# GateLoop attention and a maxout feed-forward block on one core: a shorter conversion of the weights, joined sums, constant biases, and new order lists

## The chip, the cores and the metric

The kernel runs on one core of a Trainium2 chip. The metric is the device time of one execution in microseconds. All arithmetic is in 32-bit floating point. A core has a matrix engine (TensorE, PE in the profile), three elementwise engines (VectorE or DVE, ScalarE or ACT, GpSimd or POOL) and SyncE (SP), which here only issues transfers. Transfers run on 16 DMA engines; they are issued from SP's queue and, where the transfer adds to its destination, from POOL's.

## The reference

Two blocks follow each other. The first is a gated linear recurrence over 768 steps for 4 batches and 8 heads of width 48, with complex gates:

```
mag = sqrt(a_re*a_re + a_im*a_im)
scale = minimum(mag, 0.999) / (mag + 1e-06)
a_re_n, a_im_n = a_re*scale, a_im*scale
for t in range(S):
    S_re, S_im = ar*S_re - ai*S_im + k_t (x) v_t, ar*S_im + ai*S_re
    y[:, :, t] = q_t . S_re
```

The second takes y as 3072 rows of 384 features:

```
h = maximum(maximum(x @ w1, x @ w2), x @ w3)      # 384 -> 768
out = h @ w_out                                    # 768 -> 384
```

The four weight matrices arrive as 64-bit floating point numbers.

## The kernel before, in words

The work is cut into 12 groups of 128 time steps, each for two batches (`g` 0 to 11; `x` and `y` at the end of a word name the two batches). Per group the kernel goes through these stages.

- Gates (`gates`, line 503): from the loaded `a_re` and `a_im` (words `Lr`, `Li`) the logarithm of the clamped size (`Ln`) and the angle (`w`) are made by a chain of ScalarE and VectorE words: `sqr sqi add lnL expw expe lne relu Lnop abs addw lnw expL mulai mulw stt xor half atan turn`. For group 0 they run in two halves (`sqr0`, `sqr1` and so on). `Lnop` and `addw` add one tile to another.
- Angles (`angles`, 586): `cs` is a prefix sum over time by TensorE, `t`, `nf`, `af` reduce it to one turn, `sa` and `sb` are the sines, `Cd` carries the last row into the next group by a transfer that adds.
- Turns and factors (`turns`, 622; `factors`, 687): sums of `Ln` (`sums`), their exponentials (`Ek`, `Eq`, `En`), the turned keys and queries (`uk`, `uq`), their transposes on TensorE (`tpk`, `tpq`) and copies out (`Kc`, `Qc`), per-block decay factors (`F`, `f0` to `f3`, `Q1`, `Q2`, `KB`, `QB`, `QG`, `kEn`).
- Scores, state and output of the recurrence (`scores`, 718; `state`, 770; `outputs`, 805): `A`, `B` and the picks `g0` to `g3`, `b0`, `b1`; `dk` and the state updates `h0` to `h3`; `y` and its copy `x` (`xx`, `xy`).
- Feed-forward: for groups 1 to 11 `U01 U11 U02 U12` are four stages of matrix products and `u..` the maxima (`up`, 862), and the second product is done with seven half-size products (`seven`, 897): sums `S1` to `S4` of blocks of h, products `P1` to `P7`, `Px`, `Py`, and the sums `r1 r6 r5 r7 r57 ox oy` into the output tile `ot`. Group 0 does both plainly in smaller pieces (`U01x`, `O`, `o`).

Ahead of the first feed-forward stage the weights are converted from 64 to 32 bits in 12 blocks of 384 KB (`weight_step`, 431). Block `i` is loaded raw (`WLi`), each number as two 32-bit words, and goes through the steps a (ScalarE: size of the high word, scaled), b (VectorE: an upper limit), c (VectorE: shift left by 3, in blocks 0, 3 and 6 with an or besides), e (VectorE: the upper bits of the low word or'ed in) and f (VectorE: the sign from the high word). `Wg` (blocks 1, 2, 4, 5, 7, 8) subtracts block w1 from w2 and w3 by an addition. `T`, `t`, `M`, `m` form a product of two weights; `J1` to `J4` prepare the seven products.

The order of all work is written out by hand in three lists. `SCHEDULE` (line 21) is one list of words `name:group`; each engine gets its instructions in the order of that list, and a class `Bound` (201) ties every instruction to the one in front of it on its engine. Because every instruction passes through `Bound`, the profile gives line L210 for nearly all of them, so groups are told apart by tile names. `SLOTS` (127) gives for each PSUM tile one of four double banks, in order (`banks`, 220). `OTHER` (134) names the words that are done on the second of two possible engines: a copy or size or relu or maximum on VectorE in place of ScalarE (`copy` 241, `magnitude` 248, `larger` 854), and an addition (`increase`, 255: `Lnop`, `addw`, `Wg`) on VectorE in place of an adding transfer from POOL's queue. `activation` (229) loads another table set on ScalarE whenever a word needs the set that isn't loaded: one set has the exponential and the logarithm, the other sine and arctangent. All tiles that live in turns come from tile pools with two buffers (`ldx`, `nat2`, `un2`, `fp2`, lines 189 to 194). Biases of activations stand in a tile `biases`.

Of the kernel before, what the change touches and what calls it, by code (L numbers as in the profile page):

```python
# [26 lines left out]
turn1:0 Lry:1 sqr:1 t1:0 WL11:0 Lkx:0 tx:0 nfx:0 Wa11:0 Wb10:0 csy:0 afx:0 sax:0 mkx:0 Wb11:0 Wc10:0 Lix:1 sbx:0
uqx:0 sqi:1 Lix:2 Wc11:0 Lky:0 tpqx:0 ty:0 add:1 f3x:0 f2x:0 ukx:0 Fy:0 Qcx:0 We10:0 Wf10:0 nfy:0 tpkx:0 We11:0
lnL:1 WL2:0 Q2x:0 kEnx:0 Eqy:0 expe:1 Eky:0 relu:1 xor:1 expw:1 QBx:0 Kcx:0 abs:1 T2:0 T0:0 t0:0 CL:0 KBx:0 WL1:0
Wa1:0 pw:1 Q1x:0 mky:0 Wb1:0 f0y:0 f1y:0 Wc1:0 t2:0 f2y:0 Wf11:0 lne:1 Lnop:1 Ax:0 g0x:0 Lry:2 g1x:0 We1:0 g2x:0  # L30
half:1 Lqy:0 Cdx:0 f3y:0 Liy:2 Lvx:0 mqy:0 Wa2:0 Wb2:0 lnw:1 expL:1 M0:0 mulw:1 Wc2:0 M1:0 mulai:1 dkx:0 Wf1:0
# [5 lines left out]
Wb7:0 Wg4:0 U11x:0 xor:2 By:0 dky:0 U02x:0 Lvx:1 b1y:0 h1y:0 b0y:0 QGy:0 yy:0 addw:2 lnw:2 expL:2 xy:0 U11y:0 Wg5:0
u02x:0 U02y:0 afx:1 half:2 u11x:0 Wc7:0 lne:2 We7:0 mulw:2 mulai:2 sbx:1 h2y:0 Z4:0 sax:1 h3y:0 stt:2 atan:2 Wf7:0
U12x:0 u12x:0 say:1 sby:1 Cdy:1 WL8:0 Cdx:1 turn:2 ukx:1 uqx:1 U01y:0 u01y:0 u11y:0 Wa8:0 U12y:0 csy:2 ty:2 u12y:0
csx:2 tpqx:1 tx:2 u02y:0 Qcx:1 nfy:2 Lnop:2 nfx:2 tpkx:1 Fy:1 kEnx:1 Wb8:0 Wc8:0 We8:0 Kcx:1 Wg7:0 Wf8:0 U21y:0  # L40
Wg8:0 KBx:1 f0y:1 u21y:0 Lky:1 Lqy:1 mky:1 afy:2 sumsx:2 dkx:1 Q1x:1 f1y:1 f2y:1 f3y:1 Enx:2 U21x:0 u21x:0 afx:2
# [10 lines left out]
xx:2 By:2 u02:1 Ay:2 S1:1 nfy:3 relu:4 tx:3 expe:4 S2:1 expw:4 P5:1 P6:1 g0y:2 afy:3 say:3 sby:3 nfx:3 sbx:3 g1y:2
afx:3 sax:3 abs:4 dky:2 P1:1 Lqy:3 g2y:2 g3y:2 b1y:2 J4:0 QGy:2 P7:1 Px:1 P2:1 b0y:2 h0y:2 h1y:2 ukx:3 tpkx:3 lne:4
Lnop:4 r1:1 Liy:5 mky:3 h2y:2 h3y:2 S4:1 Kcx:3 uqx:3 yy:2 Lqx:4 kEnx:3 mqy:3 tpqx:3 Qcx:3 P3:1 r6:1 xy:2 Py:1 r5:1
r7:1 P4:1 Fy:3 uky:3 r57:1 f0y:3 f1y:3 xor:4 half:4 oy:1 ox:1 Q1x:3 addw:4 dkx:3 h1x:3 Lvy:3 f2y:3 f3y:3 h0y:3
h2x:3 sumsx:4 Ekx:4 h3x:3 lnw:4 QGx:3 expL:4 Eqx:4 Fx:4 KBx:3 U11:2 Dx:1 QBx:3 mulai:4 Q2x:3 f2x:4 Enx:4 u11:2
# [88 lines left out]
def kernel(  # L145
# [15 lines left out]
    P = 128  # L161
# [881 lines left out]
```

## Time and profile before

| what | value |
|---|---|
| time, median of 3 runs | 561.11 us (557.43 to 561.78) |
| span of the profiled execution | 556.9 us |
| TensorE busy | 524.6 us |
| VectorE busy | 490.4 us in 770 instructions |
| ScalarE busy | 370.0 us |
| GpSimd busy | 74.4 us |

The span is counted from the first to the last instruction of one profiled execution; the three runs were timed apart from it and lie 0.5 to 4.9 us above it. In the lines that follow a group reads: line, engine, operation, destination tile <- source tiles, shape, count, then busy time in us and the mean of one in ns, then the idle time of the engine just before them and what ended it. In the table of stretches each engine has its busy time and its number of instructions; then come TensorE's granted clock, the mean busy share of the DMA engines and GB/s.

### The profile page before, as it was taken

To read this page: it belongs to the slowest core of one execution; us is meant where nothing else is said; L and a number is where in the kernel's file an instruction comes from. 1 tells how busy PE (TensorE), PEld (TensorE's weight loads), DVE (VectorE), ACT (ScalarE), POOL (GpSimd) and SP (SyncE) were. 2 spreads that over 40 slices of the span, in tenths; PEclk is the share of its full clock that TensorE was granted. 3 is DMA by queue.
4 is the path that set the end of the run, shared out by engine and by line. 5 is a ranking of instruction groups with operands and counts; after the bars stand their busy time and mean duration, and the time that the engine had idled before them with its cause. 6 is when DMAs were issued, how large, how long until landed. Compare 5 with 4: busy or idle time off the path is not lost.

```text
span 556.9 us, 22739 instructions
## 1 busy us (share of the span) xinstructions
PE 524.6 (94%) x10086; PEld 449.0 (81%) x10086; DVE 490.4 (88%) x770; ACT 370.0 (66%) x652; POOL 74.4 (13%) x117
## 2 busy tenths in 40 slices
PE   1669799989999999999999999999999999999997
PEld 0356588778888898888988888988888888998986
DVE  5999999989998899999988897999999999886524
ACT  5999989867965867787766858777646855530100
POOL 8105250002030001000120200120010020000000
PEclk9869999999999999999999999999999999999999
DMA  8977976456055164235364136542361144000000
GB/s 218 287 191 156 206 154 102 78 105 123 18 108 109 21 123 77 48 63 92 68 115 82 33 61 121 110 88 50 58 126 31 32 88 82 10 31 2 7 25 29
DMA packets 142530, 49.09 MB, mean 88 GB/s; under 512 B 130528, under 2 KB 135648, under 8 KB 142432
## 3 DMA queue, kind: packets, MB, share of 16 engines
q1 hardware_dynamic: 136272, 37.77, 31.9%
q0 software_dynamic: 6160, 9.87, 10.4%
q8 instruction: 79, 1.29, 1.0%
q14 instruction: 19, 0.16, 0.1%
HBM read 33.03 MB, written 4.72 MB: 68 GB/s over the span
## 4 chain that ended last, share of the span: by engine, by line
PE 84%; DVE 6%; DMA 4%; SPq 2%; issue 1%; ACT 1%; POOL 0%; DVEq 0%
PE up L210 34%; PE op L210 24%; PE y L210 7%; PE A L210 5%; PE tp L210 4%; PE dk L210 4%; PE sums L210 3%; PE cs L210 2%; SPq L210 2%; DMA xhx<-in_moe_w_out_dram 2%; PE F L210 2%; DVE xhx L210 1%; PE B L210 1%; DMA k<-in_k_dram 1%; DMA ar<-nf 1%
## 5 line engine op out<-in xcount | busy, mean ns | idle before, releaser
L210 PE MATMUL up<-xhx,w 128*128 128x256 f32 x792 | 177.4, 382 | 0.1
L210 PEld LDWEIGHTS up<-xhx,w 128*128 128x128 f32 x792 | 148.6, 190 | 21.5 <-PE B L210 0.3
L210 ACT ACT_TABLE_LOAD x45 | 57.7, 1283 | 1.5 <-PEq L1027 0.8
L210 ACT COPY atm<-B 32x128 f32<-32x128 f32 x96 | 24.5, 255 | 36.9 <-DVE atm L210 22.9
L210 PE MATMUL op<-wo,xhx 128*128 128x192 f32 (+1 forms) x220 | 48.5, 364 | 0.0
L210 DVE TENSOR_TENSOR Q<-Q,f 112x1024 f32<-112x1024 f32 (+1 forms) x48 | 45.4, 950 | 0.8 <-ACT Q L210 0.6
L210 ACT ACTIVATE f<-F 48x232 f32<-48x232 f32 x96 | 34.4, 359 | 13.2 <-PE F L210 5.4
L210 POOL DMA_DIRECT2D ar<-nf x40 | 34.2, 1280 | 65.3 <-DVE ar L210 54.7
L210 PE MATMUL y<-atm,vb 128*32 128x64 f32 x1152 | 39.4, 221 | 1.4 <-issue 1.1
L210 PEld LDWEIGHTS op<-wo,xhx 128*128 128x128 f32 x220 | 36.5, 190 | 4.3 <-DVE q L210 0.3
L210 POOL DMA_DIRECT2D Ln<-e x11 | 11.1, 1005 | 214.6 <-ACT e L210 53.9
L210 PE MATMUL y<-QG,g 112*32 112x64 f32 x1408 | 38.4, 219 | 0.9 <-issue 0.8
L210 PEld LDWEIGHTS y<-atm,vb 128*32 128x32 f32 x1152 | 32.5, 109 | 6.4 <-issue 3.6
L210 PEld LDWEIGHTS y<-QG,g 112*32 112x32 f32 x1408 | 34.8, 109 | 1.3 <-issue 1.0
L210 DVE TENSOR_TENSOR ot<-ot,op 128x192 f32<-128x192 f32 (+1 forms) x67 | 27.1, 413 | 9.0 <-PE op L210 4.3
L210 PE MATMUL op<-wo,strassen 128*128 128x192 f32 x176 | 33.0, 331 | 0.0
L210 PE MATMUL A<-Q,K 112*32 112x80 f32 x1536 | 31.6, 234 | 1.3 <-DVE Q L210 1.3
L210 DVE COPY_PREDICATED atm<-masko,A 128x256 f32<-128x256 uint8 x72 | 31.2, 435 | 1.6
L210 PE MATMUL op<-w,strassen 128*128 128x192 f32 x176 | 32.5, 329 | 0.0
L210 PEld LDWEIGHTS A<-Q,K 112*32 112x32 f32 x1536 | 27.2, 110 | 5.0 <-issue 1.9
L210 ACT COPY Q<-tp 112x1024 f32<-112x1024 f32 x23 | 23.3, 1013 | 10.3 <-PE tp L210 10.0
L210 ACT COPY ot<-op 128x192 f32<-128x192 f32 (+1 forms) x13 | 4.5, 342 | 38.2 <-PE op L210 38.2
(151 smaller groups left out, 1120.8 us busy)
## 6 DMA issues: line engine op xcount, KB each, us to landing
ar<-in_a_re_dram SPq DMA_DIRECT2D x24, 192.0 KB, 3.7
ai<-in_a_im_dram SPq DMA_DIRECT2D x24, 192.0 KB, 3.8
q<-in_q_dram SPq DMA_DIRECT2D x96, 48.0 KB, 2.6
k<-in_k_dram SPq DMA_DIRECT2D x96, 48.0 KB, 2.9
vb<-in_v_dram SPq DMA_DIRECT2D x96, 48.0 KB, 3.1
out_dram<-ot SPq DMA_DIRECT2D x23, 192.0 KB, 2.8
Ln<-e POOLq DMA_DIRECT2D x11, 384.0 KB, 4.7
w<-L POOLq DMA_DIRECT2D x9, 384.0 KB, 4.7
```

Source lines behind the costliest of these rows:

```text
L210: ins = f(*a, **kw)
```

## The change

Five things change at once.

1. The conversion of a weight block has four steps in place of five. Step b comes first and limits the high word from both sides on VectorE, reading it from the raw block; step a is then a Prelu on ScalarE that scales positive and negative numbers by different powers of two, so that the sign ends in the top bit after the shift; c is the plain shift; e writes the destination; f is gone.
2. The sums `r5` and `r7` become one instruction `r75` over both halves.
3. The biases of sine, relu and logarithm are given as constants; the tile `biases` keeps one column.
4. The tiles of the pools `ldx`, `nat2`, `un2` and `fp2` become fixed pairs, chosen by the batch. `Ek` and `Eq`, which shared one pair, get a pair each.
5. `SCHEDULE`, `SLOTS` and `OTHER` are new from the first word to the last. The new list has 1880 words (1903 before). It begins with the second half of group 0, and the constants `CL` stand first. In `OTHER`, `Lnop` of the groups 1, 3, 6, 8 and 11 and `Wg4` are new, so these additions move from POOL's transfers to VectorE; `relu:1`, `abs:1`, `afx:0`, `xx:0`, `u21x:0`, `relu:3` move from ScalarE to VectorE, and further on some copies `Kc` and `Qc`, while others go the other way.

The lists cut to the stretch that the prediction speaks of, and the code:

```diff
 SCHEDULE = """
-Lrx:0 Lix:0 sqi0:0 WL0:0 sqr0:0 xor0:0 add0:0 Wa0:0 Wb0:0 Wc0:0 We0:0 Liy:0 Wf0:0 lnL0:0 expw0:0 expe0:0 relu0:0
...
-Bx:1 KBy:1 kEny:1 lne:3 Ox:0 Eky:2 b1x:1 Eny:2 QBy:1 b0x:1 h0y:1 ukx:2 By:1 Eqy:2 yx:1 g3y:1 xx:1 b1y:1 Lqy:2 mqy:2
-Lvx:2 ox:0 Lky:2 mky:2 b0y:1 tpkx:2 expw:3 Kcx:2 uqx:2 Lnop:3 uqy:2 tpqx:2 Qcx:2 QGy:1 dky:1 h1y:1 kEnx:2 sumsx:3
-uky:2 Ekx:3 h2y:1 Eqx:3 Enx:3 yy:1 xy:1 Fy:2 f3y:2 h3y:1 dkx:2 f2y:2 abs:3 KBx:2 h0x:2 h1x:2 Q1x:2 f0y:2 f1y:2
-U11:1 u11:1 tpky:2 Kcy:2 Lky:3 QBx:2 QGx:2 addw:3 Lqx:3 h2x:2 mqx:3 h3x:2 xor:3 half:3 Cdx:2 tpqy:2 Qcy:2 Q2x:2
...
+CL:0 Zf:0 Liy:0 sqi1:0 Lry:0 sqr1:0 add1:0 lnL1:0 expe1:0 expw1:0 relu1:0 lne1:0 Lnop1:0 WL0:0 Lrx:0 Wb0:0 Lix:0 WL6:0
...
+sqr:3 tpqx:2 Qcx:2 f0x:2 U22x:0 Ay:1 By:1 dky:1 add:3 g0y:1 u22x:0 Ox:0 lnL:3 expw:3 expe:3 mky:2 g1y:1 g2y:1 relu:3
+h1y:1 uky:2 h2y:1 g3y:1 b1y:1 abs:3 lne:3 ukx:2 J1:0 QBx:2 Lnop:3 h3y:1 b0y:1 ox:0 Lry:4 Dy:0 Lvx:3 Lrx:4 Lky:3 Lqy:3
+Lvx:2 tpkx:2 tpky:2 tpqy:2 yy:1 Qcy:2 Kcy:2 xor:3 Kcx:2 Q2x:2 addw:3 h0x:2 kEny:2 Q1x:2 half:3 sumsy:3 Fy:2 xy:1 f3y:2
+Eky:3 f2y:2 lnw:3 Eqy:3 expL:3 f0y:2 mulai:3 mulw:3 sqi:4 QGx:2 stt:3 sqr:4 Eny:3 atan:3 Cdx:2 Cdy:2 kEnx:2 U11:1 u11:1
...
+P3:11 r75:11 ox:11 P4:11 r57:11 oy:11 Dx:11 Dy:11
...
-        if step == "a":
-            activation(out=ex.bitcast(FP), in_=high.bitcast(FP), func=AF.Abs, scale=2.0 ** -112)
-        elif step == "b":
-            dve.tensor_single_scalar(out=ex.bitcast(FP), in_=ex.bitcast(FP), scalar=LAST, op=OP.min)
+        if step == "b":
+            dve.tensor_scalar(out=ex.bitcast(FP), in0=high.bitcast(FP), scalar1=LAST, scalar2=-LAST, op0=OP.min,
+                              op1=OP.max)
+        elif step == "a":
+            activation(out=ex.bitcast(FP), in_=ex.bitcast(FP), func=AF.Prelu, alpha=-2.0 ** 32,
+                       scale=-2.0 ** -112 if i in (0, 3, 6) else 2.0 ** -112)
         elif step == "c":
-            if i in (0, 3, 6):
-                dve.tensor_scalar(out=ex, in0=ex, scalar1=3, scalar2=-0x80000000, op0=OP.logical_shift_left,
-                                  op1=OP.bitwise_or)
-            else:
-                dve.tensor_single_scalar(out=ex, in_=ex, scalar=3, op=OP.logical_shift_left)
+            dve.tensor_single_scalar(out=ex, in_=ex, scalar=3, op=OP.logical_shift_left)
         elif step == "e":
-            dve.scalar_tensor_tensor(out=ex, in0=low, scalar=29, in1=ex, op0=OP.logical_shift_right, op1=OP.bitwise_or)
-        elif step == "f":
-            dve.scalar_tensor_tensor(out=dst.bitcast(I32), in0=high, scalar=-0x80000000, in1=ex,
-                                     op0=OP.bitwise_and, op1=OP.bitwise_xor)
+            dve.scalar_tensor_tensor(out=dst.bitcast(I32), in0=low, scalar=29, in1=ex, op0=OP.logical_shift_right,
+                                     op1=OP.bitwise_or)
...
-                activation(out=e, in_=e, func=AF.Ln, scale=1e-6 * math.exp(-LNMAX), bias=least)
+                activation(out=e, in_=e, func=AF.Ln, scale=1e-6 * math.exp(-LNMAX), bias=math.exp(-LNMAX))
...
-            E = T[name, x] = nat2.tile([P, DM], FP, tag=name[:1 + (n == 1)], name=name[:1 + (n == 1)])
+            E = T[name, x] = es[name][c]
...
+                if name == "r75":
+                    two_ = ot.rearrange("p c n -> p (c n)")[:, NH:3 * NH].rearrange("p (u n) -> p u n", u=2)
+                    again = yl.rearrange("p (u n) -> p u n", u=1).to_broadcast([P, 2, NH])
+                    dve.tensor_tensor(out=two_, in0=again, in1=ps[:, 1, 0:DM].rearrange("p (u n) -> p u n", u=2), op=OP.add)
+                    return
```

More of the change, by code (lines that the diff above doesn't have):

```diff
@@ L27 @@
[L27 to L31, printed above, removed]
@@ L37 @@
[L37 to L41, printed above, removed]
@@ L52 @@
[L52 to L56, printed above, removed]
@@ L107 @@
-afy:10 Eqy:10 Lqy:10 dky:9 P5:8 tx:10 lne:11 P6:8 P7:8 Ay:9 h0y:9 nfx:10 h1y:9 By:9 QGy:9 h2y:9 h3y:9 g0y:9 sbx:10
-g1y:9 g2y:9 relu:11 afx:10 sax:10 ukx:10 g3y:9 P1:8 S4:8 r1:8 say:10 sby:10 mqy:10 r6:8 r5:8 r7:8 b0y:9 b1y:9
-expw:11 Py:8 P4:8 r57:8 Px:8 uqx:10 yy:9 xy:9 Fy:10 abs:11 f2y:10 Lky:10 oy:8 tpkx:10 kEnx:10 tpqx:10 f0y:10 f1y:10
-f3y:10 uqy:10 Qcx:10 Lnop:11 P2:8 Dy:8 mky:10 Kcx:10 Q1x:10 addw:11 QGx:10 Lvx:10 P3:8 ox:8 U11:9 QBx:10 u11:9
-sumsx:11 Enx:11 sumsy:11 half:11 uky:10 tpqy:10 Ekx:11 Q2x:10 Eqx:11 Lkx:11 tpky:10 Qcy:10 Kcy:10 Q2y:10 mkx:11
@@ new lines @@
+h2y:9 r6:8 r75:8 S4:8 r57:8 h3y:9 QGy:9 oy:8 sumsy:10 Fy:10 Fx:10 P2:8 P3:8 addw:11 Eqy:10 Eky:10 uqx:10 xor:11 ukx:10
+mky:10 f2x:10 f1x:10 Eny:10 mqy:10 uqy:10 ox:8 f3x:10 f3y:10 lnw:11 f0x:10 yy:9 xy:9 expL:11 f0y:10 f1y:10 tpkx:10
+tpqx:10 Qcx:10 Lnop:11 half:11 kEnx:10 mulw:11 U11:9 u11:9 U01:9 u01:9 f2y:10 Q1x:10 Kcx:10 QGx:10 uky:10 QBx:10 Cdy:10
+Cdx:10 Dx:8 Lky:11 Dy:8 Lvy:11 Lvy:10 Lqy:11 Lqx:11 Lvx:11 Lkx:11 tpqy:10 tpky:10 sumsx:11 sumsy:11 Kcy:10 Ekx:11 Eqx:11
+Enx:11 dkx:10 Q2x:10 h0x:10 Qcy:10 mulai:11 stt:11 kEny:10 Ax:10 Eky:11 Eqy:11 atan:11 Eny:11 g0x:10 g1x:10 Q2y:10
@@ L138 @@
+Kcx:9 Qcy:9 afy:10 abs:11 Lnop:11 Kcx:10 Qcy:10 Qcy:11 u11:10 xx:11
 """.split())
```

240 lines of the change are left out of this document (125 added, 115 removed).

## The prediction, made before the run

> **What bounds the kernel now.** I read the page's busy shares and its forty slices first, then a table of four stretches, then the chain of work that ended last, and only then the groups that the change touches.
>
> ```profile
> span 556.9 us, 22739 instructions
> PE 524.6 (94%) x10086; PEld 449.0 (81%) x10086; DVE 490.4 (88%) x770; ACT 370.0 (66%) x652; POOL 74.4 (13%) x117
> ...
> PE   1669799989999999999999999999999999999997
> ...
> DVE  5999999989998899999988897999999999886524
> ```
>
> ```profile
> core 0: us, PE busy (x) PEld busy (x) DVE busy (x) ACT busy (x) POOL busy (x), PEclk, DMA share, GB/s
> 0.00:112.00 112.00, 85.99 (x1436) 62.08 (x1440) 104.44 (x169) 98.49 (x173) 34.41 (x69) 0.94 0.78 174
> 112.00:124.00 12.00, 10.36 (x440) 9.02 (x429) 10.56 (x18) 8.35 (x18) 0.84 (x1) 1.00 0.45 83
> 124.00:540.00 416.00, 414.89 (x8156) 365.67 (x8155) 368.09 (x572) 262.83 (x460) 39.17 (x47) 1.00 0.36 68
> 540.00:557.00 17.00, 13.35 (x74) 12.19 (x72) 7.33 (x14) 0.32 (x1) 0.00 (x0) 1.00 0.07 24
> ```
>
> Two regimes. From 124 to 540 us TensorE is busy 414.89 of 416 us; the order of the others' work costs nothing there. In the first 112 us VectorE is busy 104.44 (7.6 idle), ScalarE 98.49, and TensorE is fed as they deliver. So the span is TensorE's work plus what it lost in the head plus a tail.
>
> ```profile
> 76.80 7.12 PE up L210 x60
> ...
> 93.19 5.81 PE op L210 x18
> ...
> 100.04 1.24 PE A L210 x64
> ...
> 117.37 1.67 PE y L210 x100
> 119.04 1.12 issue
> ...
> 122.00 4.08 PE up L210 x18
> ...
> 146.78 2.80 PE op L210 x16
> ...
> 542.96 10.40 PE op L210 x60
> ```
>
> This is the chain: start, length, what. Its last stop of TensorE in the head lies inside `yy:1` (1.12 us); behind it comes `U11:1` at 122.00. I gave each TensorE word of the list its length from such pieces and added. Ahead of `U11:1` stand twelve up words of the first group (five of them 7.12, so 17.0), two outputs (5.81 each, 11.6), three weight products 12.0, four y 6.0, four A (1.24 each) 5.0, seven sums and six cs 9.3, ten transposes 5.2, four pw and wt stages 7.4, five dk 4.5 and the small F and B 4.0: 82 us. An up stage of a later group is 4.08, a Strassen product half of the 2.80. So TensorE had lost 122.0 - 82 = 40 us by then, and loses next to nothing afterwards. The matmuls are the same in both kernels, one for one. The question is only what becomes of these 40 us.
>
> **What VectorE must do first, by the two lists.** The rows of the words that differ:
>
> ```profile
> L210 DVE TENSOR_TENSOR uk<-uk,En 128x768 f32<-128x768 f32 x24 | 22.8, 951 | 1.8 <-PE tp L210 1.7
> ...
> L210 DVE TENSOR_TENSOR g<-g,f 112x384 f32<-112x384 f32 x40 | 21.9, 552 | 2.3 <-ACT g L210 2.0
> ...
> L210 DVE TENSOR_TENSOR QB<-Q,f 112x512 f32<-112x512 f32 x24 | 16.4, 683 | 0.0
> ...
> L210 DVE SCALAR_TENSOR_TENSOR w<-w,ar 128x768 f32<-128x768 f32 x11 | 10.5, 952 | 1.9 <-ACT w L210 1.8
> ...
> L210 DVE TENSOR_SCALAR xhx<-xhx 128x768 f32<-128x768 f32 x12 | 7.5, 621 | 2.8 <-ACT xhx L210 2.7
> ...
> L210 DVE SCALAR_TENSOR_TENSOR xhx<-w,xhx 128x768 int32<-128x768 int32 x4 | 3.8, 955 | 0.1
> ...
> L210 DVE COPY xhx<-y 128x384 f32<-128x384 f32 x5 | 2.8, 556 | 1.9 <-PE y L210 1.8
> L210 DVE TENSOR_SCALAR af<-nf 128x384 int32<-128x384 int32 x8 | 2.7, 353 | 0.1
> ...
> L210 DVE TENSOR_TENSOR hT<-hT,up 128x256 f32<-128x256 f32 x6 | 2.4, 411 | 0.2 <-PE up L210 0.2
> ...
> L210 DVE TENSOR_SCALAR Ln<-L 128x768 f32<-128x768 f32 x4 | 2.2, 551 | 0.0
> ```
>
> ```profile
> 22.65 0.55 DVE L210 TENSOR_SCALAR xhx<-xhx 128x768 f32<-128x768 f32 x1
> 23.12 0.55 DVE L210 SCALAR_TENSOR_TENSOR w<-w,ai 128x384 f32<-128x384 f32 x1
> 23.59 0.95 DVE L210 SCALAR_TENSOR_TENSOR w<-wo,xhx 128x768 int32<-128x768 int32 x1
> ```
>
> Instructions of 0.55 start 0.47 apart: each costs its length less 0.08. Added so, the old list has 102.8 us of VectorE ahead of `yx:1`, the word that runs at 112 us (it is in front of the `yy:1` of the chain); measured busy up to 112 is 104.44, so the list is a clock good to 2%, and the time at a word is its list sum plus VectorE's 7.6 idle us.
>
> Up to `yy:1` (its last VectorE producer in each list) the new list leaves out the 12 steps f of the weights: 12 x (0.95 - 0.08) = 10.4 us. It has 14 words that the old one does not have there: five of 0.951 (`J1`, `Lnop:1`, `Lnop:3`, `Wg4`, `uky:2`), `QBx:2` 0.683, `h2y:1` and `h3y:1` 0.552, two relu 0.551, `xx:0` 0.556, `abs:1` 0.55, `u21x` 0.411 and `afx:0` 0.353, together 9.5 less 14 x 0.08 = 8.4. So 2.0 us less VectorE, while TensorE has 0.35 us more of its work behind it. That is the main term: **-2.4 us**. By the same count the point decides much: to `tpqx:3` it is 3.0 less and 1.5 us more TensorE (-4.5), to the place of `U11:1` in the list 3.3 us more (+3.3). I take `yy:1`, where the old trace shows TensorE's last stop; what `U11:1` itself needs, the copy of `yy:1`'s result, is a short ScalarE step, and no row makes it wait for the VectorE words listed ahead of it.
>
> **The other parts.**
> Step b now reads every other word of the raw weights. No row shows that in a tensor_scalar. The nearest is the same operation on contiguous words, 0.621 (lower bound); upper bound the 0.95 of an operation with two inputs. There a strided input (955: steps e and f, whose raw words lie two apart) costs nothing against none (952), so I take 0.62 and keep 12 x 0.33 = +4.0 us for the range. Step a moves behind b, one ScalarE pass as before: 0.
>
> ```profile
> L210 ACT ACT_TABLE_LOAD x45 | 57.7, 1283 | 1.5 <-PEq L1027 0.8
> ...
> L210 ACT ACTIVATE CS<-af,biases 128x384 f32<-128x384 f32 x24 | 14.4, 609 | 0.7 <-DVE af L210 0.5
> ...
> L210 ACT ACTIVATE CS<-nf 128x384 f32<-128x384 f32 x24 | 12.2, 514 | 0.6 <-DVE uq L210 0.6
> ```
>
> ```profile
> 61.21 0.43 PE L210 MATMUL y<-atm,vb 128*32 128x64 f32 x16
> ```
>
> Constant biases: the sine with a bias tile takes 609, without 514, so 24 x 0.095 = -2.3 us of ScalarE (relu and ln likewise, not summed). Changes between the two sets of tables, counted along the lists: 45 before (the row's 45), 53 after, +8 x 1.283 = +10.3 us of ScalarE, two of them ahead of `yx:0`. By list ScalarE has 5.5 us more to do before `yx:0` and TensorE 2.4 us less ahead of it, so ScalarE's own lead over TensorE grows by 3.1 us there. In the old trace `yx:0` starts at 61.21, where 29.6 us of TensorE's words stand ahead, a loss of 31.6; 34.7 still lies under the final 37.6, so it costs nothing; if that cover is gone it costs up to the 5.5 us. The ScalarE Activation LUTs page of the Trainium skill (What ACT_TABLE_LOAD costs) puts a switch at about 2.66 us, 1.38 of it a drain behind the load. The trace disagrees: the load is 1.283 and the next activation starts at its end. By the page the two early switches would cost 2.8 us more, and the loss at `yx:0` would be 37.5, level with the final one.
>
> ```profile
> L210 DVE TENSOR_TENSOR ot<-ot,op 128x192 f32<-128x192 f32 x46 | 16.1, 351 | 5.9 <-ACT ot L210 3.7 <-PE op L210 1.3
> ...
> L210 DVE TENSOR_TENSOR ot<-ot,op 128x384 f32<-128x384 f32 x21 | 11.1, 549 | 3.1 <-PE op L210 3.0
> ...
> L210 POOL DMA_DIRECT2D Ln<-e x11 | 11.1, 1005 | 214.6 <-ACT e L210 53.9 <-DVE QB L210 50.8 <-ACT xhx L210 34.8
> ```
>
> Joined sums: two of 0.351 become one of 0.549, -0.15 x 11, all past 124 us where TensorE hides them; in the tail `r75` ends under `P3` and `P4`, 0. Five of the 11 `Lnop` leave POOL's DMA queue for VectorE (+0.95 each, two in the head, counted above); `Cd` and `addw` behind them on POOL move up. Over the whole list VectorE is 1.7 us shorter, so its slack under TensorE stays. Tiles in place of pools: only Ek and Eq get room that they shared, which can loosen a wait, 0. Biases' memsets 0. The loads on SP are the same ones in another order; the first two are again a_re and a_im of one half, 0 either way, bounded by the start:
>
> ```profile
> 5.61 0.57 DVE L210 SCALAR_TENSOR_TENSOR ai<-ar,ai 128x384 int32<-128x384 int32 x1 [2.61 <-ACT L L210]
> ...
> 9.38 1.33 DVE L210 TENSOR_SCALAR xhx<-xhx 128x768 f32<-128x768 f32 x2 [2.71 <-ACT xhx L210]
> ```
>
> Of 5.3 us waited here at most the second can shrink (step b no longer waits for ScalarE), -2.7 to 0; I take 0, because `Lnop1:0` now stands ahead of it and waits for ScalarE's ln.
>
> **Sum.** 556.9 - 2.4 = 554.5 for an execution like the profiled one. The three timed runs have median 561.1, 4.2 above that span; carried over, **558.7**.
>
> **Rivals.**
> - *More gain.* From `yy:1` to `tpqx:3` the old list's VectorE sum (by producers) stays 26 to 28 us above TensorE's, the new one's falls from 26 to 21. If nothing else stops TensorE, the -4.5 is due and the start's -2.7 with it: -7.2, 553.9. For it: no stop of the old kind is left in the count. Against it: ScalarE's larger lead can make VectorE wait.
> - *ScalarE takes over the head.* In the new list ScalarE's sum is 5 to 6 us above VectorE's from `tpkx:0` to `tpky:0`; in the old one they are level. If VectorE idles for these 5.5 us, -2.4 + 5.5 = +3.1, 564.2. It decides once VectorE's idle time in the first 112 us passes 10 us. Against it: by `yy:0` VectorE's sum is the larger one again.
> - *A stop in each later group: slower.* The lists are new from end to end, and VectorE takes over more copies and `Lnop`s there. If TensorE stops once in each of the groups 2 to 11 as long as it did in `yy:1` (1.12), that is +11.2 - 2.4 = +8.8, 569.9. It decides from 8 us of TensorE idle between 124 and 540 us, where the old trace has 1.1. Against it: VectorE has 1.7 us less in all and is idle 48 of 416 us there.
> - *Step b at 0.95*: -2.4 + 4.0 = +1.6, 562.7, if its mean is over 0.85.
> - *Prelu is in neither loaded table set.* Then each of 12 steps adds one load or two, 15.4 to 30.8 us on a ScalarE that is 88% busy in the head (98.49 of 112): 574 to 590. The ScalarE Activation LUTs page of the Trainium skill (Table sets) says that a load is put ahead of any activation that needs one, and names relu and abs among those that every set holds, Prelu not. No run here shows it; against it, the old list's 45 changes are all of the row's 45 loads.
>
> **How the numbers follow.** Likeliest, -4.5 to 0 around -2.4: 0.48 (556.6 to 561.1). More gain 0.25. Step b 0.06. ScalarE 0.08. A stop in each group 0.09. Prelu 0.04. About 1%, 5.6 us, is what a measurement of this kernel can tell from no change: faster below 555.5, slower above 566.7. Faster: the 0.25 and 0.03 of the likeliest, 0.28. Slower: the stops, Prelu and the worse half of step b and ScalarE, 0.20. Within: 0.52. The range 552 to 567 leaves out the far end of each side.
>
> **What would show it.** Right: `U11:1` starts near 119.5 us and TensorE is full behind it; tensor_scalar with the raw weights as input near 0.62; 53 table loads; VectorE 7 to 8 us idle in the first 112. Wrong: a stop of TensorE past 124 us, VectorE idle over 10 us in the head, or more than 53 loads.

## The result and the profile after

The kernel after the change takes 567.4 us (median of 6 runs) against 558.4 for the kernel before (median of 6). The ratio of the fast runs, without one slow run of 573.0 us after the change, is 1.0116 with a 95% interval of 1.0072 to 1.0160, so slower by 1.2%; it is not the quotient of the two medians, which is 1.016. The prediction was 558.7, on a base of 561.1; the sum behind it was -2.4 us, what came is +9.1 by the medians and +6.5 by the ratio. The two profiled executions, which are compared from here on, lie 9.1 us apart: span 566.0 against 556.9 us.

The page of the kernel after, its head and the group of table loads:

```profile
span 566.0 us, 22646 instructions
...
PE 527.0 (93%) x10086; PEld 451.2 (80%) x10086; DVE 482.3 (85%) x756; ACT 372.3 (66%) x655; POOL 66.3 (12%) x111
...
L201 ACT ACT_TABLE_LOAD x53 | 68.0, 1283 | 1.7 <-PEq L1027 0.8
```

TensorE has the same 10086 products, VectorE has 8.1 us less to do (482.3 for 490.4), the table loads are 53 of 1.283 us. The products and the table loads are as foreseen; of VectorE's 8.1 us the prediction had counted 1.7. VectorE has less to do than was forecast, and the kernel is slower. The table of stretches of the kernel after, for the first three stretches that the prediction shows of before:

```profile
0.00:112.00 112.00, 83.28 (x1562) 64.39 (x1565) 98.90 (x164) 95.59 (x170) 28.91 (x66) 0.89 0.75 169
112.00:124.00 12.00, 9.54 (x196) 6.59 (x187) 11.97 (x19) 6.44 (x11) 0.86 (x1) 1.00 0.39 74
124.00:540.00 416.00, 412.38 (x8235) 361.01 (x8234) 364.52 (x563) 268.43 (x472) 36.57 (x44) 1.00 0.32 64
```

Two things stand here. In the first 112 us VectorE is busy 98.90, so it idles 13.1 us (7.6 before). And from 124 to 540 us TensorE idles 3.6 us (1.1 before).

`U11:1` is in both lists the first feed-forward stage behind the head, with the same work ahead of it but for one `dk` word (0.90 us) in before in place of two `tp` words (1.04 us) in after, so its start divides the span:

| | before | after | predicted |
|---|---|---|---|
| start of `U11:1` | 121.9 | 126.0 | 119.5 |
| from there to TensorE's last product | 431.4 | 436.4 | unchanged |
| from there to the end of the span | 3.6 | 3.6 | unchanged |

The head is 4.1 us later, the rest 5.0 us longer. These are the 9.1 us. "Rest" below is always the second row.

The chain of work of the kernel after, from what reaches TensorE at 111 us to the first feed-forward stage:

```profile
104.57 4.42 DMA ar<-in_a_re_dram
109.09 0.84 ACT e L201
109.94 0.90 ACT Q L201
111.14 0.46 PE B L201 x32
...
120.17 1.37 PE y L201 x84
121.54 2.76 issue
124.30 0.65 PE y L201 x28
...
126.10 11.85 PE up L201 x54
```

Two pieces are new. At 104.57 a load of `a_re` (`Lrx:3`) is on the path: ScalarE's square of it (`e`) stands ahead of `Q`, and `B` on TensorE waits for that. And the stop inside `yy:1`, by which the prediction chose the place to read VectorE's list, is 2.76 us long (1.12 before), named "issue": TensorE waits for no engine there.

### The profile page after: what moved, and what is told of

Read it like the earlier page. It is cut to its first block, busy times and chain, and to the rows that moved or that the text cites. A ratio compares the mean times of both kernels' runs of the same rounds, so it can differ in the third digit from the quotient of the medians.

```text
span 566.0 us, 22646 instructions
## 1 busy us (share of the span) xinstructions
PE 527.0 (93%) x10086; PEld 451.2 (80%) x10086; DVE 482.3 (85%) x756; ACT 372.3 (66%) x655; POOL 66.3 (12%) x111
## 4 chain that ended last, share of the span: by engine, by line
PE 63%; DVE 14%; ACT 7%; DMA 6%; SPq 5%; issue 3%; POOL 0%; DVEq 0%; ACTq 0%
PE up L201 28%; PE op L201 16%; SPq L201 5%; PE A L201 4%; PE y L201 4%; PE tp L201 3%; PE dk L201 2%; PE cs L201 2%; PE sums L201 2%; DVE atm L201 2%; DMA ar<-in_a_re_dram 2%; ACT L201 2%; DMA strassen<-in_moe_w_dram 1%; DMA w<-in_moe_w_dram 1%; DVE g L201 1%
## 5 line engine op out<-in xcount | busy, mean ns | idle before, releaser
L201 PE MATMUL up<-xhx,w 128*128 128x256 f32 x792 | 178.4, 382 | 0.3 <-DVE atm L201 0.3
L201 PEld LDWEIGHTS up<-xhx,w 128*128 128x128 f32 x792 | 148.2, 190 | 23.2 <-issue 1.1
L201 POOL DMA_DIRECT2D ar<-nf x40 | 33.9, 1237 | 142.2 <-DVE ar L201 142.2
L201 PE MATMUL op<-wo,xhx 128*128 128x192 f32 (+1 forms) x220 | 49.9, 365 | 0.1
L201 DVE TENSOR_TENSOR Q<-Q,f 112x1024 f32<-112x1024 f32 (+1 forms) x48 | 44.9, 950 | 0.2 <-ACT Q L201 0.2
L201 PE MATMUL y<-QG,g 112*32 112x64 f32 x1408 | 39.0, 221 | 2.8 <-issue 2.8
L201 ACT ACTIVATE f<-F 48x232 f32<-48x232 f32 x96 | 34.3, 358 | 10.2 <-PE F L201 5.0
L201 PE MATMUL y<-atm,vb 128*32 128x64 f32 x1152 | 40.0, 224 | 0.3 <-issue 0.3
L201 DVE TENSOR_TENSOR ot<-ot,op 128x384 f32<-128x384 f32 (+1 forms) x56 | 25.4, 463 | 16.2 <-PE op L201 8.5
L201 PEld LDWEIGHTS op<-wo,xhx 128*128 128x128 f32 x220 | 36.4, 190 | 3.5 <-DVE xhx L201 0.3
L201 DVE TENSOR_TENSOR xhx<-xhx,up 128x768 f32<-128x768 f32 x22 | 20.8, 949 | 20.3 <-PE up L201 20.3
L201 PEld LDWEIGHTS y<-QG,g 112*32 112x32 f32 x1408 | 35.4, 111 | 2.9 <-issue 2.9
L201 PEld LDWEIGHTS y<-atm,vb 128*32 128x32 f32 x1152 | 33.3, 112 | 4.4 <-issue 2.8
L201 ACT COPY atm<-B 32x128 f32<-32x128 f32 x96 | 24.5, 255 | 18.4 <-DVE atm L201 8.1
L201 PE MATMUL A<-Q,K 112*32 112x80 f32 x1536 | 32.6, 238 | 3.1 <-DVE Q L201 2.9
L201 PEld LDWEIGHTS A<-Q,K 112*32 112x32 f32 x1536 | 28.2, 112 | 7.2 <-DVE Q L201 3.0
L201 PE MATMUL op<-wo,strassen 128*128 128x192 f32 x176 | 32.7, 329 | 0.0
L201 DVE COPY_PREDICATED atm<-masko,A 128x256 f32<-128x256 uint8 x72 | 31.2, 434 | 1.3
L201 PE MATMUL op<-w,strassen 128*128 128x192 f32 x176 | 32.1, 328 | 0.0
L201 PEld LDWEIGHTS op<-w,strassen 128*128 128x128 f32 x176 | 29.0, 190 | 1.3 <-ACT En L201 0.3
L201 PEld LDWEIGHTS op<-wo,strassen 128*128 128x128 f32 x176 | 28.9, 190 | 1.0 <-DVE strassen L201 0.5
```

The costliest lines, as they stand in the source:

```text
L201: ins = f(*a, **kw)
```

## The experiments

In all of them the lines shift, so that the helper's line is L201 to L210. Products that an experiment adds go to parts of a PSUM tile that are written again before they are read, or read by nothing.

**The parts of the change apart.** First the new conversion in the list of before (its steps in the order b, a, c, e, the words `Wf` taken out, and the constant biases with it), then the reverse: the old conversion in the list of after.

```diff
 # e1: before.py with the new weight_step
-Lrx:0 Lix:0 sqi0:0 WL0:0 sqr0:0 xor0:0 add0:0 Wa0:0 Wb0:0 Wc0:0 We0:0 Liy:0 Wf0:0 lnL0:0
+Lrx:0 Lix:0 sqi0:0 WL0:0 sqr0:0 xor0:0 add0:0 Wb0:0 Wa0:0 Wc0:0 Liy:0 We0:0 lnL0:0
...
 # e2 and e18: after.py with the old weight_step
-WL0:0 Lrx:0 Wb0:0 Lix:0 WL6:0
+WL0:0 Lrx:0 Wa0:0 Lix:0 WL6:0
...
-lne0:0 Wc0:0 We0:0 Wb6:0
+lne0:0 Wc0:0 We0:0 Wf0:0 Wa6:0
```

> The kernel before with its own lists, pools and joins, and only two parts of the change: the four-step conversion of the weights (step b stands where a stood, a where b stood, c where e stood, e where f stood) and the constant biases. Theory 1 (the recorded one: VectorE's list sum sets the head): VectorE has 12 x 0.87 = 10.4 us less to do before yy:1, so U11:1 starts near 112 us in place of 122.0 and the time falls by about 10 us, to 548. Theory 2 (the head is bound by waits between engines, loads and ScalarE, and TensorE's last stop in yy:1 is a page of its instructions that arrives late): most of the 10.4 us becomes idle time of VectorE; U11:1 gains 2 to 5 us, the time 553 to 557.

Measured: 566.2 us, ratio 1.0120 [1.0052, 1.0189]; `U11:1` at 129.9, rest 431.1. The first stretch of e1:

```profile
0.00:112.00 112.00, 80.79 (x1372) 59.05 (x1373) 88.03 (x147) 91.80 (x164) 32.14 (x68) 0.92 0.76 170
```

VectorE has up to 10.4 us of work less (the prediction's count of the steps f) and idles 24.0 us; TensorE reaches `U11:1` 8 us later than before. The rest keeps the old pace, to 0.4 us. Neither theory came (548 and 553 to 557 us): less work for VectorE doesn't bring the head forward here, it is later. Two lines of e1 bear on the 8 us, one of ScalarE's waits up to 112 us and one of TensorE's up to 140:

```profile
ACT xhx L207 <- DVE xhx L207: 8.3, 5, 2.6
```

```profile
PE y L207 <- issue: 3.5, 2, 2.5
```

In the new order of the steps ScalarE (a) waits for VectorE (b); neither before nor after has that wait in these 112 us. And TensorE stops 3.5 us inside `y` for no engine, where before has 1.1; these are stops at page edges, which come up under TensorE's instructions below.

> The changed kernel with its own lists, and only the conversion of the weights as it was: five steps, a ahead of b, f right behind e. Theory 1 (VectorE's sum): 12 x 0.87 = 10.4 us more of VectorE ahead of yy:1, U11:1 near 136 us, the time 10 us above the changed kernel's. Theory 2 (waits bind the changed head, where VectorE is idle 13 us of 112): the idle time takes up half of it, the time 4 to 6 us above the changed kernel's.

Measured: 583.3 us, ratio 1.0407 [1.0336, 1.0477]. One execution of e2, the profiled one, took 2966.7 us; it is left out, and its trace with it. The others lie 16 us above the kernel after, more than either theory gave. The same kernel was looked at once more at the end, as e18:

> The changed lists with the old five-step conversion once more, for its profile. If VectorE's sum is what the changed head cannot spare: VectorE busy 110 of the first 112 us and U11:1 at 136 to 142. If waits between engines are: VectorE still idle 8 us or more there, with U11:1 as late.

Measured: 583.6 us; `U11:1` at 135.8, rest 442.4. Its first stretch:

```profile
0.00:112.00 112.00, 75.26 (x1232) 56.80 (x1233) 98.10 (x160) 86.09 (x152) 28.06 (x66) 0.83 0.70 160
```

VectorE has the steps f to do besides, and is yet busy 98.10 of these 112 us, less than the 98.90 of the kernel after: it waits 13.9 us, and the head is 10 us later. In the new list the new conversion is worth 16 us, in the old one (with the constant biases) it costs 5. List and conversion belong together, and their effects can't be added.

**TensorE's instructions.** The stops named "issue" were the next suspect. Counting products, weight loads and the sequencer's own instructions from the start, the stop of before at 120.16 us comes after 3488 + 33 = 3521 of them, that at 228.81 after 7802 + 71 = 7873, those of after (124.30 and 483.29) after 3521 and 17857. All four are 193 more than a multiple of 256. The page has a queue for instructions (the same row in both kernels but for the share):

```profile
q8 instruction: 79, 1.29, 0.9%
```

79 packets of 16 KB. Counting 256 to a page, TensorE's 20300 instructions are 79 pages. In the kernel after the edge ahead of `yy:1` is passed at 118.8 us, the packet starts at 121.94, ends at 122.90, and TensorE goes on at 124.30; in before the packet ended at 118.86 and TensorE went on at 120.16. If a late page of instructions is what stops TensorE, extra instructions by the half page move every edge into other words, and whole pages move none. A call of the kernel's product is two products and two weight loads, four instructions; the first expectations count it as one or two.

```diff
 # e3 (e4: 100), after.py, at csy:0
+            for _ in range(32 if T["word"] == "csy:0" else 0):
+                mm(out=ps[0:L64, 0:4], lhsT=upto[:, 0:L64], rhs=upto[:, 0:4], start=True, stop=True)
...
 # e7 (e8: 4; e10: 1), before.py, at csx:0, 32 calls a turn
+            for _ in range(2 if T["word"] == "csx:0" else 0):
```

> The changed kernel with 32 tiny matrix products (64 instructions with their weight loads, under 1 us) put into the PSUM bank of csy:0 while TensorE waits there for 6.5 us anyway. They change no result; they move the place at which TensorE crosses from one page of 256 instructions to the next. In both traces each long stop of TensorE without a named cause stands at the same count of its instructions, modulo 256, and ends 1.3 to 1.4 us after a packet of 16 KB on the instruction queue. Theory 2 (page of instructions late): the edge moves out of yy:1's burst of short instructions, the stop of 2.76 us in yy:1 goes, U11:1 starts 2.5 to 2.8 us earlier, and the time falls by 2 to 3 us. Theory 1 (VectorE or another producer stops yy:1): the stop stays, no change.

Measured: 589.8 us, ratio 1.0540 [1.0456, 1.0624]; `U11:1` at 129.6, rest 450.9. The added instructions are 128, half a page, not what the text counts. A gain was expected; it is 22 us above the kernel after, with 17.9 us of stops at page edges.

> The control of the run before: the same products, 100 of them (200 instructions). By the page theory the edge now falls 56 instructions into the transposes ahead of yy:1, and the next one at yy:1's end: a stop of 2 to 3 us stays, at the edge of the new count (behind yy:1 in place of inside it), and the time is within 1 us of the changed kernel's. If no page is involved, the stop stays inside yy:1 where it was.

Measured: 603.5 us, ratio 1.0776 [1.0714, 1.0838]; `U11:1` at 146.3, rest 452.7. 400 instructions are a page and 144, again near the half. The products stood in front of `csy:0` and held it up, so the head tells nothing here; the rest agrees with e3.

> The kernel before, with 64 small products (128 instructions of TensorE with their weight loads, some 1 us) put ahead of csx:0 in its own PSUM bank, where TensorE waits 3.2 us anyway. They change no result and no other engine's work. Theory of the pages: TensorE's instructions come in pages of 256; an edge can be crossed no sooner than some 3.6 us after the edge ahead of it. With the start times of the kernel before, the edges where they lie leave 0.9 us of shortfall in all; moved by 128 instructions they would leave 24 us (3.3 us of latency: 18). So the time rises by 15 to 24 us, all of it in stops that end 1.3 to 1.5 us after a packet of the instruction queue. Theory without pages: no change beyond 1 us.

Measured: 559.5 us, ratio 0.9983 [0.9949, 1.0016]; `U11:1` at 122.4, rest 430.4. It was in fact a whole page of 256, and it changes nothing that stands clear of the noise.

> The same with twice the products: 256 instructions, a whole page, some 2 us in the same wait of 3.2 us. Theory of the pages: every later edge falls on the same instruction as in the kernel before, so the time is within 2 us of it, though twice as much was put in. If instead the added work or its place costs, it is slower than the run with 128.

Measured: 563.4 us, ratio 1.0039 [1.0004, 1.0074]; `U11:1` at 127.1, rest 430.4. Two whole pages: the rest doesn't change. In the head the stops at page edges sum to 6.1 us (1.1 in before), which is most of what it is later by.

> The kernel before with 32 calls of a small product ahead of csx:0. The runs so far showed that one such call is two products and two weight loads, so the run with 64 calls had put in 256 instructions, a whole page, and that with 128 calls two pages; neither moved the time by more than 0.4 per cent. This one puts in 128, half a page: least work of the three. Theory of the pages (an edge no sooner than 3.6 us behind the one ahead): the shortfalls grow from 0.9 us to 24 us (18 with 3.3 us), the time rises by 15 to 24 us, and U11:1 itself starts within 4 us of where it was. Without pages: no change, as half of the work of a run that showed none.

Measured: 582.1 us, ratio 1.0379 [1.0308, 1.0450]: +20.5 us, as expected of pages; `U11:1` at 127.1, 5.2 us later where less than 4 was expected; rest 449.8. TensorE's waits from 124 to 540 us in e10, longest first:

```profile
PE dk L210 <- issue: 5.0, 4, 2.0
PE y L210 <- issue: 4.4, 5, 1.5
PE tp L210 <- issue: 2.1, 2, 1.1
PE F L210 <- issue: 1.8, 3, 0.9
```

and the same view of before and of after, their first rows:

```profile
PE y L210 <- issue: 0.8, 1, 0.8
```

```profile
PE y L201 <- issue: 3.0, 2, 2.8
PE tp L201 <- DVE g L201: 1.5, 2, 1.2
PE dk L201 <- PE B L201: 0.5, 1, 0.5
```

The columns are the total, how often, the longest. Over its whole span e10 stops 21 times, 21.2 us in all, each time at 193 past a multiple of 256. The stops hit `y`, `dk`, `tp`, `F`: words of short instructions. One whole page added costs nothing, two cost 2.2 us, half a page costs 20. The page "Runtime: NRT & Kernel Launch" of the Trainium skill (Instruction fetch mechanics) gives the 16 KiB and the 256 instructions, with which these runs agree, and calls the cost of an edge mostly hidden; here it is 2.76 us at one edge in after and 21 us over the whole of e10, and the runs decide.

**The granted clock.** After has half clock for 23.9 us of its products in the head, before for 13.7. Two kernels fill TensorE's early idle time with more products.

```diff
 # e11: after.py (e6 alike, with other counts and wider products)
+        warm()
...
+    WARM = {"csy:0": 36, "T0:0": 14, "Ay:0": 14}
+    def warm():
+        for _ in range(WARM.get(T["word"], 0)):
+            mm(out=T["ps"][:, 0, 0:P], lhsT=ident, rhs=ident, start=True, stop=True)
```

> The changed kernel with 21 dummy products of 128x128 by 128x512 ahead of csy:0 (12), T0:0 (4) and Ay:0 (5), in PSUM banks that these words own, where TensorE waits for 6.5, 2.8 and 2.9 us anyway. They change no result. In the changed kernel's profile the granted clock is 0.5 for 23.9 us (three stretches, the last around 64 to 71 us), before for 13.65. Theory: the half clock follows the idle stretches and costs the head 1 to 3 us; then these stretches shrink and the time falls by 1 to 3 us. Rival: other engines bind the head there, and the time stays within 1 us (or rises by what the dummies delay).

Measured: 592.7 us, ratio 1.0557 [1.0522, 1.0593]; half clock 10.2 us, rest 458.0. The 21 calls of e6 are 84 instructions; page stops sum to 21.6 us and hide what the clock did.

> The changed kernel with 64 calls of a 128x128 by 128x128 dummy product (256 instructions, a whole page, so that no later edge moves) in the banks of csy:0 (36), T0:0 (14) and Ay:0 (14), where TensorE waits. It keeps TensorE busy in the stretches after which the granted clock was 0.5. If the half clock costs the head: its 23.9 us shrink below 12 and the time falls by 1 to 3 us. If it costs nothing there: the clock rises all the same and the time stays within 1.5 us.

Measured: 575.3 us, ratio 1.0258 [1.0173, 1.0342]; half clock 6.8 us, `U11:1` at 130.6, rest 439.4. The mean clock rose from 0.979 to 0.994 and nothing was gained: TensorE waits for the others in the head, and the added products made `csy:0` late, so that VectorE waited 5.5 us for `t` behind it. Whether a fill that delays nothing would gain wasn't tried.

**Who holds the head.** Waits of the kernel after up to 112 us (up to 124 for the queue), of VectorE, ScalarE and SP's queue:

```profile
DVE L L201 <- ACT e L201: 4.1, 3, 3.0
DVE Ln L201 <- ACT e L201: 2.5, 1, 2.5
```

```profile
ACT e L201 <- DMA ar<-in_a_re_dram: 5.8, 4, 2.0
```

```profile
SPq L201 <- POOL vb L201: 5.4, 1, 5.4
```

VectorE waits for ScalarE's `e`, ScalarE for loads of `a_re`, and SP's queue stands 5.4 us for POOL and `vb`. Two `vb` tiles are cleared by POOL (words `Z2`, `Z3`) before `Lvx:1` may load into one. POOL's timeline, after and then before:

```profile
73.05 2.62 POOL L201 DMA_DIRECT2D w<-w  x2 [1.16 <-DVE w L201]
75.02 1.57 POOL L201 DMA_DIRECT2D Ln<-e  x1
75.60 2.41 POOL L201 MEMSET vb<- 128x768 f32 x2
```

```profile
53.87 2.29 POOL L210 MEMSET vb<- 128x768 f32 x1
...
56.30 2.06 POOL L210 MEMSET vb<- 128x768 f32 x1
```

In the new list they stand behind `Wg7`, `Wg5` and `Lnop:2`, adding transfers that wait for their operands: 20 us later than before. SP then issues back to back until 104 us, and `Lrx:3` is among the last. Two cures:

```diff
 # e5: the loads earlier
-Lky:0 Lrx:1
+Lrx:1 (behind Lry:1)
-Lqy:2 Lrx:3 Lry:3 yx:1
+Lvy:1 Lrx:3 Lry:3 Lix:4
...
 # e9: the clearing earlier
-mqx:1 Lnop:2 Z2:0 Z3:0 U02y:0
+m1:0 Z2:0 Z3:0 lnL:2
```

> The changed kernel with three loads put further ahead in its list: Lrx:1 beside Lry:1 (ahead of the raw weights WL9 and of Lky:0), and Lrx:3 Lry:3 ahead of Lix:4, Liy:4 and Lqy:2. Theory 2 (the changed head loses its time in waits): add:1 on VectorE and sqr:3 on ScalarE (2.0 us idle for that load) no longer wait, TensorE's stop of 1.68 us ahead of By:1 goes, U11:1 starts 1.5 to 3 us earlier and the time falls by 1.5 to 3 us. Rival (other waits stand right behind): the stops move, less than 1 us.

Measured: 574.9 us, ratio 1.0220 [1.0186, 1.0255]; `U11:1` at 130.7, rest 441.6. Slower: the load moved up stood at the head of SP's queue until 102.3 us (104.1 in the kernel after), and the load of `q` stood behind it:

```profile
DVE q L203 <- DMA q<-in_q_dram: 7.5, 2, 6.8
```

So an earlier place in the list did not make the load early, and what an early load would be worth isn't shown by this run. What was ahead of it in the queue was left.

> The changed kernel with two words of its list moved: Z2:0 and Z3:0, two memsets of v's tiles on GpSimd, stand right behind m1:0 in place of behind Wg7, Wg5 and Lnop:2. In the changed kernel's trace they run at 75.6 us, behind adding transfers that wait for VectorE on the same queue, and SP holds the load Lvx:1 for 5.4 us for them, with all loads of the groups 2 and 3 behind it. Theory 2 (SP's queue binds the changed head): SP goes on some 5 us earlier, q, k and a_re of groups 2 and 3 land earlier, TensorE's stop of 1.68 us ahead of By:1 goes, the time falls by 1.5 to 4 us. Rival (their buffers are not free any earlier, or other waits stand behind): under 1 us.

Measured: 567.4 us, ratio 1.0123 [1.0058, 1.0188]; `U11:1` at 120.7, 5.4 us earlier than after, but rest 441.2, 4.8 longer. Two stretches of e9, its ScalarE's wait for `a_re` up to 112 us, two pieces of its chain:

```profile
0.00:112.00 112.00, 86.92 (x1602) 66.89 (x1603) 102.37 (x171) 96.76 (x171) 29.15 (x66) 0.91 0.75 169
...
124.00:540.00 416.00, 409.65 (x8147) 358.30 (x8146) 363.64 (x561) 264.81 (x466) 34.73 (x42) 1.00 0.32 63
```

```profile
ACT e L203 <- DMA ar<-in_a_re_dram: 1.6, 2, 1.3
```

```profile
117.75 1.18 issue
...
120.73 11.85 PE up L203 x54
```

The wait for `a_re` falls from 5.8 to 1.6 us, VectorE's idle time from 13.1 to 9.6, and the same page's stop from 2.76 to 1.18. e15, e16 and e17 below have the same list up to `U11:1` and start it at 121.9 to 122.6. So two clearings in POOL's queue cost the head 3.4 to 5.4 us; 1.6 of the 5.4 passed through the page. At the end nothing is left of it: TensorE now idles 6.4 us between 124 and 540, with two stops that the kernel after doesn't have in this length, and behind them, from 373.1 us on, the granted clock is 0.5 for 3.4 us:

```profile
PE y L203 <- ACT atm L203: 2.5, 1, 2.5
PE tp L203 <- DVE g L203: 1.9, 1, 1.9
```

It would be wrong to call these stops the price of the earlier head. e5, whose `U11:1` starts 4.6 us later than after's, has the same two:

```profile
PE y L203 <- ACT atm L203: 2.7, 1, 2.7
...
PE tp L203 <- DVE g L203: 1.6, 2, 1.3
```

e11 has them too (1.6 and 2.1 us), e18 the second (1.9) and one of 3.1 us for `g` in place of the first. With the new order behind `U11:1` and no stops at page edges added, the rest was 436.4 us in after and 439.4 to 446.4 in five more runs (e5, e9, e11, e12, e18), with an earlier head and with later ones.

**The additions on VectorE.** Seven of them (with `addw:5`, which is new in `OTHER` as well) back to POOL's transfers, in the new list:

```diff
-relu:1 abs:1 Lnop:1 xx:0 Wg4:0 ... Lnop:3 ... addw:5 ... Lnop:6 ... Lnop:8 ... Lnop:11
+relu:1 abs:1 xx:0 ...
```

> The changed kernel with its own order, but the additions Lnop of the groups 1, 3, 6, 8, 11, addw of group 5 and Wg4 as adding transfers on GpSimd's queue, as in the kernel before. VectorE has 7 x 0.87 = 6 us less. If the small stops of TensorE behind U11:1 (rest of the span 436.4 us against 431.4 before) are due to the work that VectorE took over: the rest falls by 2 us or more. If they are due to the order: no change there, or longer, as the list was written for additions by VectorE.

Measured: 583.8 us, ratio 1.0410 [1.0341, 1.0479]; `U11:1` at 131.5, rest 446.4. In this order the additions on VectorE are worth 16 us, head and rest both.

**The rest, by a seam.** The new head up to a word, then the list of before for what is left. e13 and e14 cut at `U11:1`, with and without the clearing of e9; e15 cuts at `U01:2`, e16 at `U12:1`, e17 at `csx:4`, all three with it. In e13 and e14 one half of the last group's output lacks one of its sums.

```diff
 # H = head of the new list up to the cut + words of the old list that are left
-U11:1 u11:1 U01:1 KBx:2 ...        (new order to the end)
+sumsx:3 Ekx:3 Eqx:3 Enx:3 dkx:2 KBx:2 h1x:2 f1y:2 U11:1 u11:1 ...  (old order to the end)
```

> The changed kernel (its code, conversion, constant biases, fixed tiles, joined r75) with its own list up to U11:1, the two memsets moved ahead, and behind it the words of the former list in the former order, with the former PSUM banks and the former choice of engines there. If the order behind U11:1 is what takes the head's gain back: U11:1 at about 120.7, the rest 430 to 432 us as before (436 to 441 in the changed list), the span 553 to 555 and the time 1 per cent under the kernel before. If the rest is bound by something else (the conversion's code, tables, pages): the rest stays near 436 to 441 and the time at 567.

Measured: 573.9 us, ratio 1.0238 [1.0191, 1.0285]; `U11:1` at 136.9, rest 431.4. TensorE's longest wait from 60 to 200 us in e13, at the joint:

```profile
PE dk L204 <- ACT En L204: 11.2, 1, 11.2
```

> The same without moving the memsets: U11:1 near 126 as in the changed kernel, the rest 430 to 432, the time 5 us above the run with the memsets moved, so level with the kernel before or up to 4 us slower. If memsets make no difference here either: the same time as that run.

Measured: 574.1 us, ratio 1.0229 [1.0162, 1.0295]; `U11:1` at 140.7, rest 430.7. The joint is bad, since the old list has done words by then that the new one has not; they now stand ahead of `U11:1`. By the medians (573.9 and 574.1) the clearing makes no difference at this joint; the profiled execution of e14 is its slowest, 577.8. But the rest is the old 431 from either start, so what lengthens it in after is the order (the list, the banks and the choice of engines) behind `U11:1`, not the conversion's code.

> The changed kernel with the memsets moved ahead and its own list up to U01:2 (a group behind U11:1, so that nothing of the seam waits for ScalarE); behind it the words of the former list in the former order with the former banks (two at the seam differ) and choice of engines; in the last group P7 and r75 stand ahead of ox. If the changed order behind U11:1 takes the head's gain back: U11:1 at 120.7, the rest 431 to 434 us, the span 552 to 555, the time 0.5 to 1.5 per cent under the kernel before. If the rest is bound by something that both lists share: 436 to 441 and no gain.

Measured: 562.9 us, ratio 1.0063 [1.0037, 1.0089]; `U11:1` at 121.9, rest 435.6. Two stretches of e15:

```profile
124.00:200.00 76.00, 73.48 (x1448) 64.04 (x1447) 65.64 (x99) 52.35 (x89) 9.12 (x11) 0.98 0.34 65
200.00:540.00 340.00, 339.80 (x6729) 300.37 (x6728) 298.51 (x460) 210.04 (x376) 29.09 (x35) 1.00 0.34 66
```

The seam costs 2.5 us, behind it TensorE loses 0.2 in 340. The tail stops once more for 1.2 us (`P4` waits for VectorE's `ot`). It is the best version of the changed code found, 4.5 us under the kernel after, and doesn't reach the kernel before.

> The same with the seam at U12:1, right behind U01:1: less of the changed list, more of the former. U11:1 at 120.7; if the seam is free of waits, the rest 431 to 434 us and the time as in the run with the later seam; a stop of a few us at the seam (dkx:2 or its neighbours for ScalarE, as in the first hybrid, 11 us) would show there.

Measured: 571.3 us, ratio 1.0216 [1.0173, 1.0260]; `U11:1` at 122.6, rest 442.3: 8 us of stops at its seam.

> The run with the later seam, with U01:2 and P4:1 of the changed list still ahead of the seam (they cover tpkx:3's wait) and P4:11 ahead of r75:11 and ox:11 in the last group. If the order is the bound: the two stops at the seam and the one at the end shrink by 2 to 3.5 us, the span 557.5 to 559, the time 559.5 to 561, level with the kernel before. If they reappear elsewhere: 562 to 564.

Measured: 566.6 us, ratio 1.0110 [1.0066, 1.0155]; `U11:1` at 121.9, rest 437.2. The tail's stop is gone, but there are about 5 us of stops at the seam. A joint without stops was not found.

## Why the prediction was wrong

**The main term, -2.4 us.** The step that failed is "the list is a clock good to 2%, and the time at a word is its list sum plus VectorE's 7.6 idle us", with its choice of `yy:1`, "where the old trace shows TensorE's last stop". Both halves are wrong.
- That stop was no wait for VectorE. It falls on a page edge of TensorE's instructions; e10 makes twenty more like it by adding half a page. The profile of before had said "issue", not an engine, and the prediction read past it.
- The 7.6 idle us are no constant. VectorE idles 13.1 us in after, 13.9 in e18 and 24.0 in e1, and `U11:1` came later each time, with fewer words for VectorE (after, e1) or without (e18). The sum of a list dates a word only while the engine does not wait.

What the head cost instead is shown by e9: two clearings of `vb` behind adding transfers in POOL's queue, SP's queue 5.4 us behind them, late loads of `a_re`, ScalarE and VectorE behind those. With them moved `U11:1` starts at 120.7, 1.2 us from the predicted 119.5, and in e15 to e17 at 121.9 to 122.6, where before has 121.9. The prediction did say that on SP the loads are "the same ones in another order" and costed that at 0 by the kernel's start alone; it did not ask which POOL word each load waits for, or where that word had gone.

**"The order of the others' work costs nothing there"** (124 to 540 us) is the second step that failed. It was true of the old list. With the new list the rest is 5.0 us longer, and e13, e14, e1, e7 and e8 have the old 430 to 431 wherever `U11:1` starts. The rival "a stop in each later group" had the right kind and the wrong size: TensorE idles 3.6 us there, not the 8 from which it was to decide, in small stops. That its sum, +8.8, is close to the +9.1 is luck: it is made of +11.2 in the rest and -2.4 in the head, and 5.0 and 4.1 came. The table of stretches from the start of `U11:1` to TensorE's last product, after and then before:

```profile
126.03:562.42 436.39, 432.42 (x8276) 378.63 (x8268) 369.85 (x571) 269.78 (x474) 36.06 (x44) 1.00 0.31 61
```

```profile
121.93:553.35 431.42, 430.31 (x8240) 379.69 (x8236) 376.72 (x586) 264.56 (x464) 40.01 (x48) 1.00 0.35 66
```

Of the 5.0 us, 2.9 are idle time (436.39 - 432.42 = 4.0, against 1.1), among them the tail's 0.6 where `P4` waits for `ot`, which was costed at 0; 2.1 are TensorE's busy time. The 36 more products in the row don't make them, since by the two words named above they come to -0.1; the same products took longer, and the runs do not explain it. In e9 this part also swallows the gain of the head, 5.4 us earlier at `U11:1` and 0.5 at the last product; but as it is as long in e5 and e18, whose heads are late, that the earlier head brings the stops is not shown.

**The ScalarE rival.** Its sign came (VectorE idle over 10 us in the head), and so did the direction. Its reason came only in part: 4.2 of the 5.8 us that ScalarE waited for `a_re` go with e9, so a late load, not the longer list, was most of it: of VectorE's 5.5 us of added idle time 3.5 go with it.

**What held.** Step b, of which the prediction asked whether a strided input is dearer, on VectorE's timeline of the kernel after:

```profile
33.29 0.55 DVE L201 TENSOR_SCALAR xhx<-w 128x768 f32<-128x768 f32 x1
34.60 0.56 DVE L201 TENSOR_SCALAR xhx<-w 128x768 f32<-128x768 f32 x1 [0.76 <-DMA w<-in_moe_w_dram]
```

0.55, and 0.59 in the mean of all twelve, against 0.62 before and far from 0.95. The table loads are exactly 53, so Prelu adds none, and that rival is out; its worry was that the ScalarE: Activation LUTs page of the Trainium skill (Table sets) names relu and abs among what every set holds, and Prelu not. The load is 1.283 us and the next activation starts at its end (77.08 + 1.28, then 78.38).

**What stays open.** Which chain of VectorE and ScalarE sets the pace of the new rest is not settled: the waits there name `g`, `B`, `atm`, `Eq`, `QB` and `ot` in after and `uk` in e15, and no run took one away alone. Whether the new head with a clean joint would beat the kernel before is open too: 120.7 plus 431.4 would make 1.3 us less than before, but that is only added up, and with the 121.9 to 122.6 of e15 to e17 nothing is left of it. All starts and lengths are of one profiled execution each, while the runs of one kernel lie up to 8 us apart (556.4 to 564.4 for before, beside e1), so differences of 1 us or so tell nothing by themselves.

## What to carry to other kernels

Before dating a word by an engine's list sum, look at what stands in front of it in the in-order queues, those of the transfers too: one clearing behind an adding transfer held SP's queue, and through it two engines. A gain at the front need not reach the end (5.4 us became 0.5 in e9), so compare the start and the length of each part, not the end alone. And when a profile names "issue" for TensorE, count its instructions by 256: bursts of short ones on a page edge cost up to 3.4 us each here (e3), and any change in their number ahead that is not whole pages moves all later edges.

## What was not expected of the hardware

A kernel whose TensorE is full can lose 20 us to the phase of its instruction pages alone: +20.5 us for 128 small added instructions, about 0 for 256 (e10, e7). The wait at one and the same edge, inside `yy:1`, was 1.12, 1.18 and 2.76 us in before, e9 and after; in after the packet started 3.2 us after the edge ahead of it. Raising the granted clock from 0.979 to 0.994 gained nothing in e11, where TensorE waits for others and the added products held one of them up.
